# Attention with memory feeding a gated expert layer: the first group of tokens is made of two batches' ends, and attended tokens are transposed one pair of heads at a time

## Chip, cores and metric

One core of a Trainium2 chip. The metric is the device time of one execution in microseconds (us), taken as the median of several runs; lower is better.

## What is computed

```python
# attention with memory: B=4 batches, H=8 heads, S=576 tokens, D=64
scores = causal(scale * q @ k.T)              # per head, 576 x 576, masked
a = softmax(scores)
local = a @ v
mem_out = phi(q) @ M_prev / (phi(q) @ z_prev + 1e-6)
x = g * mem_out + (1 - g) * local             # g = sigmoid(beta), one number for each head
# expert layer over all 2304 tokens: d_model 512, d_ff 1536
x = x.transpose(0, 2, 1, 3).reshape(2304, 512)
out = (sigmoid(x @ w_gate) * (x @ w_val)) @ w_out
```

The expert weights arrive as 64-bit floats. The kernel turns each value into a sum of two 32-bit numbers (hi and lo) and multiplies with three products: hi*hi, hi*lo, lo*hi.

## The kernel before

The 2304 tokens are worked off in six **groups** of 384 tokens (`NG`, `GT`). Groups 0 to 3 are *plain*: the first 384 tokens of one batch each. Groups 4 and 5 are *tail* groups: the last 192 tokens of two batches each. In a group attention runs over four **pairs** of heads (n = 0 to 23 in all, four to a group). A pair has three items c, each of 128 tokens. In a plain pair the items see 128, 256 and 384 keys. In a tail pair items 0 and 1 see 512 keys and item 2, half from each batch, sees 576 (in pieces of 320 and 256).

For each item `scores` (line 447) multiplies queries with keys on TensorE, takes the masked maximum on VectorE (L481) and the exponential on ScalarE (L490). `turn` (495) transposes the result on TensorE (L217) and ScalarE copies it out. After the third item `values` (514) multiplies with the values (L214); four small VectorE operations and one addition give `xs`. `memory` (402) is the memory term (L214, VectorE). Scores come in two forms: pairs n < `SPLIT` = 9 multiply 32-bit numbers directly, with 64 rows to a head (L469); from pair 9 on `split` (426) makes hi and lo parts on ScalarE and VectorE (`kq`, `ql`), and TensorE takes two full-height products to a head (L477 and L478 by the helper on L210).

`across` (540) turns the finished tokens of a **whole group** so that the model dimension lies on partitions. For each of three token blocks it does four transposes, one ScalarE cast of 512 columns (`xh`) and one VectorE subtraction (`xl`). It runs after the group's fourth pair.

`moe` (656) is the expert layer of a group: for each of 12 slices f of d_ff it does 24 matmuls of 384 columns (12 for the gate, 12 for the value, on `xh` and `xl`), the *gate* on ScalarE and VectorE (tanh L694, product L696, cast, subtraction), and, one slice later, 9 matmuls of 512 columns into three accumulators (`down`). The accumulators are copied out by ScalarE (`ob`, L711) and stored. In the first group's layer the weights are loaded and converted (`convert`, 603): three thirds to a slice, each with two ScalarE and five VectorE operations of 512 columns (L611, L613, L616, L619, L233). The ring `sv` has three buffers, so conversion runs at most two slices ahead of use. Later groups read the converted weights back.

The order on each engine is made by `Program.issue` (96): every operation is recorded with a cost, and a list scheduler with fixed costs writes out one queue for each engine, by the order of recording where several operations are ready. At run time each queue is worked off in its order. First all of group 0's attention is recorded (`weights(0)` and `weights(1)` at two of its steps), then the layer of group g with the attention of group g + 1 woven in between (`SPREAD`). While group 0 is in attention all eight PSUM banks serve it; afterwards three do.

Of the kernel before, what the change touches and what calls it, by code (L numbers as in the profile page):

```python
# [21 lines left out]
VC = 66  # L22
# [123 lines left out]
def tile_attention_memory_moe(  # L146
# [75 lines left out]
    def copy(out, in_, n, r, w):  # L222
        act(n, lambda: nc.scalar.copy(out=out, in_=in_), r, w)  # L223
# [78 lines left out]
    vr_r = Ring("vr", [128, 5, 2, VC], F32, 2)  # L302
    vt_r = Ring("vt", [128, 5, 2, VC], F32, 2, {0: ("wr0", ("wr", 0)), 1: ("wr1", ("wr", 1))})
    kp_r = Ring("kp", [128, 2 * GT], F32, 4)
# [11 lines left out]
    class Pair:  # L316
        pass

    def batches(g):
        return [g] if g < B else [2 * (g - B), 2 * (g - B) + 1]  # L320

    def items_of(g):

        return [(128 * c, 128 * c + 128) for c in range(3)] if g < B else [(0, 512), (0, 512), (64, S)]

    pairs = []
    for g in range(NG):
        for p in range(HP):
            u = Pair()
            u.g, u.p, u.tail, u.bs = g, p, g >= B, batches(g)  # L330
# [8 lines left out]
    xs_t = {}  # L339

# [173 lines left out]
    def values(n):  # L514
# [5 lines left out]
        with pg.block():  # L520
            for c in range(3):
# [10 lines left out]
        if u.g not in xs_t:  # L532
            xs_t[u.g] = xs_r.take()
        xs, xk = xs_t[u.g]
        x = xs[:, :, 2 * u.p:2 * u.p + 2]
        k = xk + (u.p,)
        scaled(x, [k], pv, tk, rs_r, 1e-9, ga[:, 2 * u.p:2 * u.p + 2], "ga")
        tt(nc.vector, ALU.add, x, x, u.xm, GT, [k] + u.xm_k, [k])

    def across(g, c):  # L540

        xs, xk = xs_t[g]
        if g not in x_t:
            x_t[g] = [xh_r.take(), xl_r.take(), []]
        (xh, xh_k), (xl, xl_k), keys = x_t[g]
        tp, tk = bank("att")
        x = xs[:, c].rearrange("p h d -> p (h d)")
# [3 lines left out]
        src = tp.rearrange("p (a q) -> p a q", a=KD)  # L551
        hi, lo = xh[:, :, c * 128:c * 128 + 128], xl[:, :, c * 128:c * 128 + 128]
        kh, kl = xh_k + (c,), xl_k + (c,)
        copy(hi, src, DM, [tk], [kh])
        sub(nc.vector, lo, src, hi.bitcast(F32), DM, [tk, kh], [kl])
        keys += [kh, kl]

    seq = [(n, c) for n in range(NP) for c in range(3)]

    def attn():  # L560
# [6 lines left out]
        for t in range(len(seq) + SKEW):  # L567
# [15 lines left out]
            if t >= SKEW:  # L583
                n, c = seq[t - SKEW]
                turn(n, c)
                yield
                if c == 2:
                    values(n)
                    load_values(n + 2)
                    yield  # L590
                    if n % HP == HP - 1:
                        g = pairs[n].g
                        for c in range(3):
                            across(g, c)
                            yield
                        yield ("group", g)

# [50 lines left out]
    def rows(g, t):  # L648
        if g < B:
            return [(g * S + t * 128, 0, 128)]  # L650
        b = 2 * (g - B)
        if t < 2:
            return [((b + t) * S + GT, 0, 128)]
        return [((b + e) * S + GT + 128, 64 * e, 64) for e in range(2)]

    def moe(g):
# [16 lines left out]
        for f in range(NF):  # L673
            cur = ready_w.pop(g * NF + f)
            pz = []
            for part in range(2):
                pp, pp_k = bank("gv")
                pz.append((pp, pp_k))
                (wh, wh_k), (wl, wl_k) = cur[part]
                n = 0  # L680
                for kd in range(KD):
                    o = slice(kd * 128, kd * 128 + 128)
                    for (l, l_k), r in (((wh, wh_k), xh), ((wh, wh_k), xl), ((wl, wl_k), xh)):
                        matmul(pp[:, :GT], l[:, o], r[:, kd], GT, [l_k] + xk, [pp_k],
                               n == 0, n == 3 * KD - 1)
                        n += 1
                    if kd % 2 == 1:
                        yield
            th, th_k = th_r.take()
# [33 lines left out]
    def count(g):  # L723

        return HP * 9 + 4

# [82 lines left out]
```

## Time and profile before

| | |
|---|---|
| runs | 705.32, 705.69, 705.99 us; median 705.69 us |
| profiled execution | 704.67 us, of which the profile's span is 702.9 us |
| TensorE (PE) busy | 672.7 us, 96% of the span |
| VectorE (DVE) busy | 369.8 us, 53% |
| ScalarE (ACT) busy | 340.3 us, 48% |
| GpSimd (POOL) busy | 8.0 us, 1% |
| DMA | 122.20 MB, mean 174 GB/s |

An engine's busy share is a mean over the span; it hides that DVE is busy nearly all the time in the first quarter and a third of it at the end. "PEclk" is the clock that TensorE was granted, as a share of 2.4 GHz: 1.00 is 2.4 GHz, 0.50 is 1.2 GHz, and values between are stretches of both. A matmul's listed duration overlaps the next one's, so the cost of one in a stream is read from start to start.

### The profile page before, as it was taken

To read this page: it belongs to the slowest core of one execution; us is meant where nothing else is said; L and a number is where in the kernel's file an instruction comes from. 1 tells how busy PE (TensorE), PEld (TensorE's weight loads), DVE (VectorE), ACT (ScalarE), POOL (GpSimd) and SP (SyncE) were. 2 spreads that over 40 slices of the span, in tenths; PEclk is the share of its full clock that TensorE was granted. 3 is DMA by queue.
4 is the path that set the end of the run, shared out by engine and by line. 5 is a ranking of instruction groups with operands and counts; after the bars stand their busy time and mean duration, and the time that the engine had idled before them with its cause. 6 is when DMAs were issued, how large, how long until landed. Compare 5 with 4: busy or idle time off the path is not lost.

```text
span 702.9 us, 12510 instructions
## 1 busy us (share of the span) xinstructions
PE 672.7 (96%) x4992; PEld 598.0 (85%) x4992; DVE 369.8 (53%) x1005; ACT 340.3 (48%) x666; POOL 8.0 (1%) x52
## 2 busy tenths in 40 slices
PE   4997999998999999999999999999999999999996
PEld 3564888777899999999998988989898889999995
DVE  5866999989654444453545355363634532311111
ACT  6664565557645526543546366373736533221111
POOL 2000000000000000000000000000000000000000
PEclk9976999999999999999999999999999999999999
DMA  8654668776744345544537335534631423454542
GB/s 269 215 167 154 210 221 280 245 260 233 281 154 158 148 142 189 202 153 149 185 120 253 116 124 185 147 133 160 223 136 70 159 66 117 126 219 179 180 152 73
DMA packets 31946, 122.20 MB, mean 174 GB/s; under 512 B 7568, under 2 KB 9616, under 8 KB 22672
## 3 DMA queue, kind: packets, MB, share of 16 engines
q1 hardware_dynamic: 31888, 121.41, 49.9%
q8 instruction: 39, 0.64, 0.4%
q14 instruction: 19, 0.16, 0.1%
HBM read 104.09 MB, written 17.30 MB: 173 GB/s over the span
## 4 chain that ended last, share of the span: by engine, by line
PE 88%; ACT 5%; DVE 4%; DMA 1%; issue 1%; POOL 1%; POOLq 0%; SPq 0%; ACTq 0%; DVEq 0%
PE bank L210 68%; PE bank L214 10%; PE bank L217 7%; PE bank L469 3%; ACT kq L223 2%; ACT a L490 1%; DMA mb<-in_mz_dram 1%; DVE wt L616 1%; DVE wt L619 1%; ACT at L223 0%; DVE a L481 0%; DVE wt L611 0%; DVE wt L613 0%; DMA out_dram<-ob 0%; DVE xs L233 0%
## 5 line engine op out<-in xcount | busy, mean ns | idle before, releaser
L210 PE MATMUL bank<-xh,wg 128*128 128x384 f32 x576 | 168.9, 349 | 2.6 <-ACT wg L223 2.2
L210 PE MATMUL bank<-xh,sv 128*128 128x384 f32 x576 | 170.1, 348 | 0.0
L210 PE MATMUL bank<-sv,gh 128*128 128x512 f32 x432 | 140.7, 403 | 0.4 <-ACT gh L223 0.4
L210 PEld LDWEIGHTS bank<-xh,wg 128*128 128x128 f32 x576 | 107.0, 191 | 10.3 <-issue 3.3
L210 PEld LDWEIGHTS bank<-xh,sv 128*128 128x128 f32 x576 | 106.2, 188 | 3.1 <-issue 1.4
L696 DVE SCALAR_TENSOR_TENSOR th<-th,bank 128x384 f32<-128x384 f32 x72 | 39.8, 553 | 118.8 <-PE bank L210 117.6
L481 DVE CUSTOM_DVE_ANT_0 a<-bank,mask 128x128 f32<-128x128 f32 (+3 forms) x144 | 66.5, 486 | 66.8 <-PE bank L210 54.1
L490 ACT ACTIVATE a<-a,st 128x128 f32<-128x128 f32 (+3 forms) x144 | 79.8, 581 | 42.2 <-DVE st L481 41.2
L210 PE MATMUL bank<-xl,wg 128*128 128x384 f32 x288 | 99.2, 344 | 0.0
L210 PE MATMUL bank<-xl,sv 128*128 128x384 f32 x288 | 98.9, 343 | 0.0
L694 ACT ACTIVATE th<-bank 128x384 f32<-128x384 f32 x72 | 35.2, 489 | 116.1 <-PE bank L210 115.7
L210 PEld LDWEIGHTS bank<-sv,gh 128*128 128x128 f32 x432 | 78.2, 188 | 14.1 <-issue 1.4
L210 PE MATMUL bank<-sv,gl 128*128 128x512 f32 x216 | 86.6, 401 | 0.0
L223 ACT CAST gh<-th 128x384 fp32r<-128x384 f32 x72 | 36.8, 512 | 99.1 <-DVE th L696 98.8
L223 ACT COPY at<-bank 128x512 f32<-128x512 f32 (+1 forms) x120 | 59.0, 514 | 35.9 <-PE bank L217 34.5
L217 PE MATMUL bank<-idn,a 128*128 128x128 f32 x400 | 72.4, 282 | 3.1 <-ACT a L490 2.9
L223 ACT CAST kq<-kp 64x768 fp32r<-64x768 f32 (+1 forms) x92 | 56.0, 615 | 16.5 <-PE bank L210 15.2
L217 PEld LDWEIGHTS bank<-idn,a 128*128 128x128 f32 x400 | 51.3, 145 | 13.7 <-ACT a L490 5.8
L210 PEld LDWEIGHTS bank<-xl,wg 128*128 128x128 f32 x288 | 55.1, 191 | 2.6
L210 PEld LDWEIGHTS bank<-xl,sv 128*128 128x128 f32 x288 | 54.3, 189 | 0.6 <-issue 0.2
L233 DVE TENSOR_TENSOR gl<-th,gh 128x384 fp32r<-128x384 f32 x72 | 40.0, 556 | 22.4 <-ACT gh L223 21.9
L210 PEld LDWEIGHTS bank<-sv,gl 128*128 128x128 f32 x216 | 40.6, 188 | 9.4 <-issue 0.3
(62 smaller groups left out, 723.4 us busy)
## 6 DMA issues: line engine op xcount, KB each, us to landing
sv<-w SPq DMA_DIRECT2D x60, 1024.0 KB, 4.8
wr<-in_w_dram SPq DMA_DIRECT2D x36, 512.0 KB, 4.1
kp<-in_qk_dram SPq DMA_DIRECT2D x32, 384.0 KB, 4.3
w<-sv SPq DMA_DIRECT2D x12, 1024.0 KB, 5.4
out_dram<-ob SPq DMA_DIRECT2D x16, 256.0 KB, 3.9
vr<-in_vp_dram SPq DMA_DIRECT2D x16, 198.0 KB, 4.6
vt<-in_vp_dram SPq DMA_DIRECT2D x8, 330.0 KB, 3.5
vr<-in_vp_dram SPq DMA_DIRECT2D x8, 330.0 KB, 3.1
```

Source lines behind the costliest of these rows:

```text
L210: lambda: nc.tensor.matmul(out=out, lhsT=lhsT, rhs=rhs, start=start, stop=stop), r, w)
L214: lambda: nc.tensor.matmul(out=out, lhsT=lhsT, rhs=rhs, start=start, stop=stop), r, w)
L217: pe(0.110, lambda: nc.tensor.transpose(out=out, in_=in_, identity=identity), r, w)
L223: act(n, lambda: nc.scalar.copy(out=out, in_=in_), r, w)
L233: dve(n, lambda: nc.vector.tensor_tensor(out=out, in0=in0, in1=in1, op=op), r, w)
L469: pe(2 * m / 2385.0, lambda kp=kp, j=j, r=r, q=q, m0=m0, m1=m1: nc.tensor.matmul(out=sp[j][0][m0:m1, :m], lhsT=kp[r, u.qa + q:u.qa + q + m ...
L481: dve(m + 60, lambda aj=aj, sj=sj, pj=pj: nc.vector.tensor_tensor_reduce(out=aj[:, k0:k1], in0=pj[:, :m], in1=mk, scale=-0.125, scalar=3.0 ...
L490: act(W, lambda aj=aj, sj=sj: nc.scalar.activation(out=aj[:, :W], in_=aj[:, :W], func=AF.Exp, scale=-1.0, bias=sj[:, len(ns) - 1:len(ns)], ...
L616: dve(DM, lambda: nc.vector.scalar_tensor_tensor(out=t, in0=hi, scalar=-0x40000000, in1=t, op0=ALU.bitwise_and, op1=ALU.bitwise_or,), [wr_ ...
L619: dve(DM, lambda: nc.vector.scalar_tensor_tensor(out=t, in0=lo, scalar=29, in1=t, op0=ALU.logical_shift_right, op1=ALU.bitwise_or,), [wr_k ...
L694: act(GT, lambda: nc.scalar.activation(out=th, in_=pg_[:, :GT], func=AF.Tanh, scale=0.5), [pg_k], [th_k])
L696: dve(GT, lambda: nc.vector.scalar_tensor_tensor(out=th, in0=th, scalar=1.0, in1=pv[:, :GT], op0=ALU.add, op1=ALU.mult,), [th_k, pv_k], [t ...
```

## The change

Three things are changed, and lines move up by a few, so that L469 becomes L472, L481 becomes L484, L696 becomes L689.

1. The groups run in another order: `ids = [4, 0, 1, 2, 3, 5]`. The tail group of batches 0 and 1 comes first, then the four plain groups, then the other tail group. Which pairs use the direct form still goes by n < 9: before these were nine plain pairs, now four tail pairs and five plain pairs.
2. `across` runs after **each pair**, with three transposes, one cast and one subtraction of 384 columns. A pair's tokens fill one of the four parts kd of `xh` and `xl`. For f = 0 the layer's 24 matmuls are written so that kd = 0, 1, 2 of gate and value come first and the six of kd = 3 last, and each waits for its own part alone.
3. Buffers: `xs` is a ring of two small tiles in place of one large; values of even pairs go to `vt`, of odd pairs to `vr`, and `vt` no longer shares memory with the buffers of the raw weights.

```diff
-    vt_r = Ring("vt", [128, 5, 2, VC], F32, 2, {0: ("wr0", ("wr", 0)), 1: ("wr1", ("wr", 1))})
+    vt_r = Ring("vt", [128, 5, 2, VC], F32, 2)
-    xs_r = Ring("xs", [128, 3, H, D], F32, 1)
+    xs_r = Ring("xs", [128, 3, 2, D], F32, 2)
+    ids = [B, *range(B), *range(B + 1, NG)]
     def batches(g):
-        return [g] if g < B else [2 * (g - B), 2 * (g - B) + 1]
+        i = ids[g]
+        return [i] if i < B else [2 * (i - B), 2 * (i - B) + 1]
-            ring = vt_r if u.tail and n % 2 == 0 else vr_r
+            ring = vr_r if n % 2 else vt_r
-    def across(g, c):
+    def across(n):
...
-        for i in range(KD):
-            transpose(tp[:, i * 128:i * 128 + 128], x[:, i * 128:i * 128 + 128], idn,
-                      [xk + (i,), "idn"], [tk])
+        for c in range(3):
+            transpose(tp[:, c * 128:c * 128 + 128], u.x[:, c].rearrange("p j d -> p (j d)"), idn,
+                      [u.x_k, "idn"], [tk])
+        hi, lo = xh[:, u.p], xl[:, u.p]
...
-                    if n % HP == HP - 1:
-                        g = pairs[n].g
-                        for c in range(3):
-                            across(g, c)
-                            yield
-                        yield ("group", g)
+                    across(n)
+                    yield ("group", pairs[n].g) if n % HP == HP - 1 else None
...
+            turns = [(part, kd) for part in range(2) for kd in range(KD)]
+            if f == 0:
+                turns = [x for x in turns if x[1] < KD - 1] + [x for x in turns if x[1] == KD - 1]
...
-                        matmul(pp[:, :GT], l[:, o], r[:, kd], GT, [l_k] + xk, [pp_k],
-                               n == 0, n == 3 * KD - 1)
+                    matmul(pp[:, :GT], l[:, o], r[:, kd], GT, [l_k] + xk[kd], [pp_k],
+                           kd == 0 and i == 0, kd == KD - 1 and i == 2)
```

Three places where the queues differ. In the names `kp` is a pair's queries and keys, `a` the exponentials, `at` their transposes, `vr` and `vt` values, `mb` and `ph` the memory term, `wr` and `wt` raw weights in conversion, `wg` and `sv` converted ones, `th` the gate.

TensorE at the start of the program, before:

```order
L469 MATMUL bank_63<-kp_101 128x128
L469 MATMUL bank_64<-kp_101 128x128
L469 MATMUL bank_66<-kp_101 128x256
L469 MATMUL bank_67<-kp_101 128x256
L469 MATMUL bank_69<-kp_101 128x384
L469 MATMUL bank_70<-kp_101 128x384
L214 MATMUL bank_65<-mb_104,ph_105 128x130 x3
L217 MATMUL bank_68<-idn,a_107 128x128
L217 MATMUL bank_68<-idn,a_108 128x128
```

and now:

```order
L472 MATMUL bank_63<-kp_101 128x512
L472 MATMUL bank_64<-kp_101 128x512
L472 MATMUL bank_66<-kp_102 128x512
L472 MATMUL bank_67<-kp_102 128x512
L217 MATMUL bank_68<-idn,a_112 128x128 x4
L217 MATMUL bank_69<-idn,a_113 128x128 x4
L472 MATMUL bank_70<-kp_101 64x320
L472 MATMUL bank_63<-kp_101 64x320
L472 MATMUL bank_70<-kp_102 64x320
L472 MATMUL bank_63<-kp_102 64x320
```

The first pair's scores are of two batches (`kp_101`, `kp_102`) and of 512, 320 and 256 columns; the memory term, which waits for `mb`, comes 14 rows into the queue in place of six.

TensorE at the end of the first group, before, from the last pair's values to the layer's first matmuls:

```order
L214 MATMUL bank_65<-vr_106,at_136 64x66 x12
L217 MATMUL bank_70<-idn,a_118 128x128
L217 MATMUL bank_70<-idn,a_107 128x128
L469 MATMUL bank_69<-kp_101 128x384
L469 MATMUL bank_69<-kp_103 128x128
L217 MATMUL bank_66<-idn,xs_134 128x128
L217 MATMUL bank_67<-idn,xs_134 128x128
L217 MATMUL bank_68<-idn,xs_134 128x128
L469 MATMUL bank_68<-kp_101 128x256
L210 MATMUL bank_66<-xh_142,wg_89 128x384
L210 MATMUL bank_66<-xl_143,wg_89 128x384
```

and now, from the last pair's transposed tokens to the last six matmuls of f = 0 (the last pair's values end nine rows earlier, and ahead of those stand 18 of f = 0's 24 matmuls):

```order
L217 MATMUL bank_65<-idn,xs_143 128x128 x3
L472 MATMUL bank_69<-kp_102 128x256
L214 MATMUL bank_70<-vt_103,at_122 64x66 x4
L214 MATMUL bank_70<-vt_103,at_127 64x66 x8
L214 MATMUL bank_70<-vt_103,at_137 64x66 x3
L210 MATMUL bank_66<-xh_140,wg_89 128x384
L210 MATMUL bank_66<-xl_141,wg_89 128x384
L210 MATMUL bank_66<-xh_140,wg_89 128x384
L210 MATMUL bank_67<-xh_140,sv_128 128x384
L210 MATMUL bank_67<-xl_141,sv_128 128x384
L210 MATMUL bank_67<-xh_140,sv_128 128x384
```

Between the last transposes and the matmuls that need them there now stand a score matmul and the values of the next group's first pair (`vt_103`).

VectorE at the same place, before:

```order
L233 TENSOR_TENSOR xs_134<-xs_134,xm_131 128x3x128
L616 SCALAR_TENSOR_TENSOR wt_140<-wr_127,wt_140 128x512
L613 TENSOR_SCALAR wt_126<-wt_126 128x512
L619 SCALAR_TENSOR_TENSOR wt_140<-wr_127,wt_140 128x512
L233 TENSOR_TENSOR xl_143<-bank_66,xh_142 128x4x128
L233 TENSOR_TENSOR xl_143<-bank_67,xh_142 128x4x128
L233 TENSOR_TENSOR xl_143<-bank_68,xh_142 128x4x128
```

and now, with the first gate (`th`) behind it:

```order
L233 TENSOR_TENSOR xs_143<-xs_143,xm_135 128x384
L398 TENSOR_SCALAR rn_136<-bank_70 128x6
L400 RECIPROCAL rn_136<-rn_136 128x6
L233 TENSOR_TENSOR rn_136<-rn_136,gs 128x6
L233 TENSOR_TENSOR xm_135<-bank_70,rn_136 128x384
L484 ISA a_118,st_120<-bank_69,mask 128x256
L484 ISA st_120 128x1
L233 TENSOR_TENSOR xl_141<-bank_65,xh_140 128x384
L391 SCALAR_TENSOR_TENSOR ph_126<-kp_106,ph_126 128x384
L689 SCALAR_TENSOR_TENSOR th_147<-th_147,bank_67 128x384
```

The last pair's `xl` is one subtraction of 384 columns in place of three of 512, with the next group's attention ahead of it in place of weight conversion.

## Rows read from the trace of the kernel before

**Rows 1.** Windows between first copies of finished accumulators; busy us (instructions), clock, DMA.

```profile
core 0: us, PE busy (x) PEld busy (x) DVE busy (x) ACT busy (x) POOL busy (x), PEclk, DMA share, GB/s
180.32:277.93 97.61, 97.61 (x724) 90.92 (x723) 48.77 (x143) 48.55 (x100) 0.43 (x4) 1.00 0.48 173
277.93:379.90 101.97, 101.97 (x739) 94.25 (x738) 50.48 (x139) 50.23 (x101) 0.46 (x4) 1.00 0.47 169
379.90:504.60 124.70, 123.26 (x1057) 112.07 (x1057) 62.31 (x167) 67.52 (x127) 0.93 (x8) 1.00 0.45 158
504.60:620.47 115.87, 114.83 (x1004) 105.30 (x1004) 44.76 (x120) 47.76 (x89) 0.47 (x4) 1.00 0.36 127
620.47:695.69 75.22, 75.22 (x397) 70.58 (x396) 13.37 (x24) 13.85 (x27) 0.00 (x0) 1.00 0.46 164
```

**Rows 2.** Windows of the early part, from DVE's first operation on.

```profile
5.49:30.68 25.19, 20.48 (x174) 14.11 (x174) 20.24 (x74) 19.07 (x44) 0.33 (x3) 1.00 0.78 248
30.68:46.00 15.32, 12.22 (x83) 8.02 (x79) 11.52 (x37) 8.91 (x18) 0.11 (x1) 0.68 0.66 220
46.00:61.93 15.93, 11.26 (x95) 7.39 (x93) 13.40 (x40) 8.44 (x18) 0.22 (x2) 0.82 0.39 118
61.93:73.72 11.79, 11.79 (x47) 9.52 (x47) 6.42 (x18) 5.90 (x13) 0.00 (x0) 0.64 0.48 167
73.72:175.27 101.55, 97.63 (x659) 81.41 (x657) 94.55 (x233) 62.08 (x121) 0.66 (x6) 0.98 0.73 246
175.27:180.32 5.05, 5.05 (x27) 3.62 (x27) 3.96 (x14) 4.27 (x9) 0.00 (x0) 1.00 0.72 188
```

**Rows 3.** Timeline of PE and DVE around 35 us: start us, us, engine, line, operation.

```profile
35.03 0.42 DVE L613 TENSOR_SCALAR wt<-wt 128x512 int32<-128x512 int32 x1
35.37 0.55 DVE L481 CUSTOM_DVE_ANT_0 a<-bank,mask 128x384 f32<-128x384 f32 x1
...
36.63 0.90 PE L217 MATMUL bank<-idn,a 128*128 128x128 f32 x3 [2.70 <-ACT a L490]
```

**Rows 4.** Timeline of PE at the end of the first group.

```profile
60.78 1.22 PE L469 MATMUL bank<-kp 64*128 64x256 f32 x2 [2.43 <-DVE xl L233]
61.93 0.69 PE L210 MATMUL bank<-xh,wg 128*128 128x384 f32 x1
```

**Rows 5.** Timeline of PE: direct scores and transposes in the first group's attention.

```profile
8.31 2.93 PE L469 MATMUL bank<-kp 64*128 64x128 f32 x12 [8.31 <-DMA kp<-in_qk_dram]
...
21.62 0.91 PE L469 MATMUL bank<-kp 64*128 64x384 f32 x2
22.46 0.66 PE L217 MATMUL bank<-idn,a 128*128 128x128 f32 x4
23.05 0.48 PE L469 MATMUL bank<-kp 64*128 64x128 f32 x2
```

**Rows 6.** Chain that ended last: start us, us; both heads' scores, eight transposes, tail memory and values.

```profile
80.70 0.85 PE bank L469 x4
...
353.10 0.87 PE bank L217 x8
...
381.89 1.03 PE bank L214 x8
...
387.56 3.18 PE bank L214 x104
```

**Rows 7.** Timeline of PE: split scores of a tail pair.

```profile
488.31 0.39 PE L210 MATMUL bank<-kq 128*128 128x512 f32 x1
488.54 0.40 PE L210 MATMUL bank<-kq,ql 128*128 128x512 f32 x1
```

**Rows 8.** Groups by form: VectorE's masked maximum, tail and plain.

```profile
L481 DVE CUSTOM_DVE_ANT_0 a<-bank,mask 128x512 f32<-128x512 f32 x32 | 21.1, 686 | 10.6 <-PE bank L210 10.3
L481 DVE CUSTOM_DVE_ANT_0 a<-bank,mask 128x256 f32<-128x256 f32 x32 | 12.6, 414 | 5.0 <-PE bank L210 4.4 <-ACT a L490 0.4
L481 DVE CUSTOM_DVE_ANT_0 a<-bank,mask 128x320 f32<-128x320 f32 x16 | 7.2, 488 | 19.7 <-PE bank L210 19.7
```

More of the change, by code (lines that the diff above doesn't have):

```diff
@@ L317, in tile_attention_memory_moe @@
         pass
+    ids = [B, *range(B), *range(B + 1, NG)]
     def batches(g):
-        return [g] if g < B else [2 * (g - B), 2 * (g - B) + 1]
+        i = ids[g]
+        return [i] if i < B else [2 * (i - B), 2 * (i - B) + 1]
     def items_of(g):
-        return [(128 * c, 128 * c + 128) for c in range(3)] if g < B else [(0, 512), (0, 512), (64, S)]
+        return [(128 * c, 128 * c + 128) for c in range(3)] if ids[g] < B else [(0, 512), (0, 512), (64, S)]
     pairs = []
@@ L329, in tile_attention_memory_moe @@
             u = Pair()
-            u.g, u.p, u.tail, u.bs = g, p, g >= B, batches(g)
+            u.g, u.p, u.tail, u.bs = g, p, ids[g] >= B, batches(g)
             u.nk = 5 if u.tail else 3
@@ L338, in tile_attention_memory_moe @@
     x_t = {}
-    xs_t = {}
     def load_unit(g):
@@ L531, in values @@
                                     keys, [tk], i == 0, i == nb - 1)
[L532 to L538, printed above, removed]
-    def across(g, c):
[L542 to L545, printed above, removed]
-        tp, tk = bank("att")
-        x = xs[:, c].rearrange("p h d -> p (h d)")
-        for i in range(KD):
-            transpose(tp[:, i * 128:i * 128 + 128], x[:, i * 128:i * 128 + 128], idn,
-                      [xk + (i,), "idn"], [tk])
[L551 to L556, printed above, removed]
+        u.x, u.x_k = xs_r.take()
+        scaled(u.x, [u.x_k], pv, tk, rs_r, 1e-9, ga[:, 2 * u.p:2 * u.p + 2], "ga")
+        tt(nc.vector, ALU.add, u.x, u.x, u.xm, GT, [u.x_k] + u.xm_k, [u.x_k])
+    def across(n):
+        u = pairs[n]
+        if u.p == 0:
+            x_t[u.g] = [xh_r.take(), xl_r.take(), []]
+        (xh, xh_k), (xl, xl_k), keys = x_t[u.g]
+        tp, tk = bank("att")
+        for c in range(3):
+            transpose(tp[:, c * 128:c * 128 + 128], u.x[:, c].rearrange("p j d -> p (j d)"), idn,
+                      [u.x_k, "idn"], [tk])
+        hi, lo = xh[:, u.p], xl[:, u.p]
+        kh, kl = xh_k + (u.p,), xl_k + (u.p,)
+        copy(hi, tp[:, :GT], GT, [tk], [kh])
+        sub(nc.vector, lo, tp[:, :GT], hi.bitcast(F32), GT, [tk, kh], [kl])
+        keys.append([kh, kl])
     seq = [(n, c) for n in range(NP) for c in range(3)]
@@ L648, in rows @@
     def rows(g, t):
-        if g < B:
-            return [(g * S + t * 128, 0, 128)]
-        b = 2 * (g - B)
+        b = batches(g)[0]
+        if ids[g] < B:
+            return [(b * S + t * 128, 0, 128)]
         if t < 2:
@@ L674, in moe @@
             cur = ready_w.pop(g * NF + f)
[L675 to L678, printed above, removed]
-                (wh, wh_k), (wl, wl_k) = cur[part]
[L680 to L683, printed above, removed]
-                        matmul(pp[:, :GT], l[:, o], r[:, kd], GT, [l_k] + xk, [pp_k],
-                               n == 0, n == 3 * KD - 1)
-                        n += 1
-                    if kd % 2 == 1:
-                        yield
+            pz = [bank("gv") for _ in range(2)]
+            turns = [(part, kd) for part in range(2) for kd in range(KD)]
+            if f == 0:
+                turns = [x for x in turns if x[1] < KD - 1] + [x for x in turns if x[1] == KD - 1]
+            for n, (part, kd) in enumerate(turns):
+                pp, pp_k = pz[part]
+                (wh, wh_k), (wl, wl_k) = cur[part]
+                o = slice(kd * 128, kd * 128 + 128)
+                for i, ((l, l_k), r) in enumerate((((wh, wh_k), xh), ((wh, wh_k), xl), ((wl, wl_k), xh))):
+                    matmul(pp[:, :GT], l[:, o], r[:, kd], GT, [l_k] + xk[kd], [pp_k],
+                           kd == 0 and i == 0, kd == KD - 1 and i == 2)
+                if n % 2 == 1:
+                    yield
             th, th_k = th_r.take()
@@ L723, in count @@
     def count(g):
-        return HP * 9 + 4
+        return HP * 10
     constants()
```

## The prediction

> **What bounds the kernel.** I began with the time from one group's first accumulator copy to the next, since the change swaps whole groups. From 180.32 us on TensorE has nearly no gap: in each window its busy time is within 1.5 us of the window and the clock is 1.00 [rows 1]. There the kernel lasts as long as its matmuls. The five windows read as 75.2 us of expert layer (the last one, which has no attention woven in) plus the next group's attention: 97.61 and 101.97 us with a plain group, 124.70 and 115.87 with a tail group. So a plain group's attention is worth (97.61 + 101.97)/2 - 75.2 = 24.6 us there and a tail group's (124.70 + 115.87)/2 - 75.2 = 45.1 us.
>
> The early part is another matter [rows 2]. From 5.49 to 73.72 us, where VectorE does the first gate's product, VectorE is busy 20.24 + 11.52 + 13.40 + 6.42 = 51.6 of 68.2 us and TensorE 55.8, but part of that at 1.2 GHz: the granted clock is 0.68, 0.82 and 0.64 in three of the four windows. Two places show why. At 35 us VectorE works through weight conversion before it takes a masked maximum; ScalarE's exponential waits for that, and TensorE waits 2.70 us for ScalarE [rows 3]. At the end of the group TensorE waits 2.43 us behind VectorE's `xl`, and the layer begins at 61.93 us [rows 4]. From 73.72 to 175.27 us (first to twelfth gate) VectorE is busy 94.55 and TensorE 97.63 of 101.55 us: both are nearly full.
>
> **The late part.** Behind the first group's layer stand now three windows with a plain group and one with a tail group, in place of two and two. One tail attention, 45.1 us, goes out and a plain one, 24.6, comes in: **-20.5 us**. The last window (75.2) and what follows it stay, since a tail group is still last. The turning costs nothing here: the transposes are 72 as before, four casts and subtractions of 384 columns replace three of 512, and ScalarE and VectorE are busy only half of these windows [rows 1]. Without that cover it would be some tenths of a microsecond a group.
>
> **The early part** gets those matmuls instead, in the direct form. I sum what the new queues place ahead of the first gate.
>
> TensorE, one tail pair. A direct score group takes 0.84 us from start to start for 384 columns (21.62 to 22.46 us, one head) [rows 5], and 0.85 us for both heads when they stand next to each other [rows 6]. With 128 columns it is 0.41. I draw a line through these: 0.21 plus 0.21 for each 128 columns, so 1.05 for 512, 0.74 for 320, 0.63 for 256. No trace row shows two batches' 64-row halves next to each other. They could run together, as the two heads do, or singly; I take together, because a tail pair's values, half of which alternate so between batches at 64 columns, take 3.18/104 = 31 ns an instruction [rows 6]. In the new queue the four pairs' scores are then 12 groups of 512, 9 of 320 and 8 of 256: 24.3 us. Run singly they would be 16 of each, 38.7; I keep +14 for the upper end. A pair has besides 1.03 of memory, 3.18 of values and 26 + 3 transposes at 0.87/8 = 0.109 [rows 6]: 7.4. Four pairs: 24.3 + 29.6 = 53.9. The queue has also f = 0's 24 matmuls, at 0.175 (4.2), and the next plain pair with the beginning of another, about 8.5. Sum **66.6 us** from 8.31 us on, when the first queries land [rows 5]: **74.9 us** at the earliest.
>
> VectorE. To the old 51.6 us come, for four pairs, two heads each of 0.686 + 0.686 + 0.488 and about 0.48 in place of 0.414, 0.55 and 0.28, which lie on the line through 256 and 512 columns [rows 8], 1.09 x 8 = 8.7 us; two and a half more thirds of a conversion ahead of the first gate (11 finished in the new queue, 9 in the old) at an estimated 2.5 us (five operations, two of 0.34 [rows 3] and three of 0.6, as 512 columns are), 6; and a further pair's beginnings, 4. Overlaps of 0.08 a row [rows 3] take 1 off. Sum 69 from 5.49: **74.5 us**. So the two engines need the same time, where before they needed 57 (VectorE) and 49 (TensorE, the same sum over the old queue, 40.3 from 8.31), and the first gate came at 73.72, 17 us late.
>
> How late will it be now? About 9 of the 17 us belong to the end of the group: some 4 of idle time ahead of 61.93 and then 61.93 to 73.72 at a clock of 0.64, which costs about 4 more. There the changed queue has 18 of f = 0's 24 matmuls ahead of the last pair, and no triple `xl`. The other 8 lie over 45 us of group 0 and should grow with its length (66.6 against 40.3): 13. I take **14, so the first gate at 89 us**, with ends at 5 (80 us) and at 26 (101).
>
> From first to twelfth gate VectorE's queue holds 82 us in place of 93 (two or three thirds and more attention are already done), TensorE's 88 in place of 89, by the same durations. TensorE loses 12 us there now, 4 of them idle late in the window behind a full VectorE; I take **94 us** (89 to 98). With the 5.05 us that follow [rows 2] the first accumulator copy comes at 89 + 94 + 5 = 188 us, 7.7 later.
>
> In this are further edits. The split form leaves four tail pairs (512 columns take two products of 0.23 us a head [rows 7], by columns 3.9 us a pair) and comes to four plain ones; by the direct form a tail pair costs 6.1, so +8.7, and four plain pairs go from some 3.1 (1.9 where the heads stand together, 3.8 where they don't) to 1.4, so -6.8: together +1.9, which the sums above and the unchanged window lengths already carry to within 1 us. DMA: a tail pair brings four loads of 384 and 330 KB in place of two, about 3.4 MB more for the group, and on SyncE's queue they stand ahead of `mb`, so the memory term starts some 3 us later; 14 queue rows of TensorE cover most of it. The DMA share there is 0.78 and 0.66, the bytes find room; if not, `wr` lands late and ScalarE's first conversion step with it. I price that within the 14.
>
> **Sum**: +7.7 - 20.5 = -12.8 us on the profiled execution, 704.67 to 691.9. The median of the runs is 1.0 above that execution; I predict **692.9 us**.
>
> A page's rule speaks against the change. The row: four transposes take 0.59 us to the next start when 64-row scores follow [rows 5], against 0.44 by the rate of [rows 6], so going from one shape to the other costs about 0.15. The Trainium skill (TensorEngine Tiling (Array Packing), Key Properties) says that changing the tiling mode drains TensorE. By that rule the 15 additional changes ahead of the first gate (60 in the new queue, 45 in the old) are 2 us more early, and the 27 fewer behind it give 4 back; by the rows both are in the 0.21 above already.
>
> **Rivals.**
> *The early part runs at TensorE's old pace* (slower). Before, the first gate took 65.4 us from 8.31 for 40.3 us of matmuls, 1.62 each. If that ratio holds, because every pair passes TensorE, VectorE, ScalarE and TensorE again with one item of lead, then 66.6 x 1.62 + 8.3 = 116 us, the first copy at 215 and the run at 719. It decides from a first gate at about 102 us on (704.7). For it: the waits of [rows 3], which the change doesn't remove. Against it: the ratio is that of a queue with 40 us of matmuls against 50 of VectorE. Chance 0.15.
> *The same lateness as before.* 25 us behind TensorE's sum gives a first gate at 100 and 703.5 on the profiled scale, 704.5 on the median: no change. Chance 0.06. Near it lies that the turning by pairs saves nothing, since the last six matmuls of f = 0 still wait for the last pair: plus 8, a run of 700.5; this is in my forecast's range.
> *TensorE stays busy and at full clock.* First gate at 80, then 89 us: first copy at 174, the run 678 to 679. For it: the clock fell to 0.68 after the wait of [rows 3] and to 0.64 after that of [rows 4], and stood at 1.00 in every window where TensorE was full [rows 1]; the new first group has twice the matmuls. The Trainium skill (TensorE: Matmul & The Clock Gate, The HAM clock gate) says that the throttled clock is the default and activity releases it, which would bring this case about; the trace agrees in both directions. Chance 0.17.
>
> **Numbers.** My forecast (684 to 703) has 0.62. The range 680 to 704 leaves out most of the slow rival and part of the fast one. About 0.2% of the time, 1.4 us, is what a measurement can tell from no change. Faster: 0.62 + 0.17 = 0.79; within 0.2%: 0.06; slower: 0.15.
>
> **What would show it.** Right: windows behind the first copy of about 98, 102, 100, 118 and 75 us; a first gate between 80 and 101 us; layer matmuls of f = 0 ahead of the last pair's transposes and no wait for `xl` over 1 us; VectorE near 90% busy to the first gate. Wrong: a first gate past 102 us, or a clock at half for 30 us of the early part (then the rival of the old pace); a late part that saves other than 19 to 22 us (then the swap was mispriced); two batches' score halves that run singly (0.74 us for each 320-column matmul).

## The result and the profile after

The changed kernel takes **686.73 us** (median of four runs, 686.13 to 687.59) against 705.83 (705.32 to 705.99) for the kernel before in the same session: a ratio of 0.9737 (95% interval 0.9723 to 0.975), 19.1 us less. The prediction was 692.9 us, with a range of 680 to 704. The profiled execution took 686.17 us, of which 684.4 are the span.

From the page of the changed kernel: the totals, and two of the forty-slice strips.

```profile
span 684.4 us, 12496 instructions
PE 663.3 (97%) x4992; PEld 582.0 (85%) x4992; DVE 363.1 (53%) x995; ACT 334.3 (49%) x656; POOL 8.1 (1%) x52
DVE  6799889898864443454444345454445533111111
PEclk9999999999999999999999999999999999999999
```

The reader is to see the last strip: the granted clock is at 0.9 or more of 2.4 GHz in every slice. VectorE is busy for 60% and more of each of the first twelve slices, and for half or less of those behind them.

The windows of the changed kernel, cut at the same events as [rows 1, 2]: first gate, twelfth gate, first accumulator copy, and the first copies of the five layers that follow.

```profile
core 0: us, PE busy (x) PEld busy (x) DVE busy (x) ACT busy (x) POOL busy (x), PEclk, DMA share, GB/s
5.49:85.44 79.95, 72.36 (x762) 46.20 (x763) 70.17 (x212) 58.28 (x116) 1.42 (x12) 1.00 0.76 253
85.44:178.76 93.32, 92.29 (x573) 77.07 (x572) 84.29 (x206) 60.37 (x117) 0.33 (x3) 1.00 0.70 234
178.76:182.78 4.02, 4.02 (x60) 3.32 (x59) 3.86 (x10) 2.00 (x4) 0.00 (x0) 1.00 0.59 210
182.78:285.39 102.61, 102.52 (x744) 93.75 (x743) 51.10 (x152) 50.65 (x105) 0.54 (x5) 1.00 0.47 164
285.39:383.50 98.11, 98.11 (x722) 91.00 (x721) 45.03 (x132) 46.92 (x96) 0.43 (x4) 1.00 0.45 163
383.50:485.90 102.40, 102.40 (x739) 94.00 (x738) 50.07 (x140) 50.47 (x101) 0.47 (x4) 1.00 0.49 171
485.90:601.37 115.47, 114.68 (x1004) 105.27 (x1004) 45.24 (x121) 48.13 (x90) 0.47 (x4) 1.00 0.35 128
601.37:677.13 75.76, 75.65 (x397) 70.60 (x396) 13.35 (x24) 13.73 (x27) 0.00 (x0) 1.00 0.46 163
```

| stretch | before, us [rows 1, 2] | after, us | change | forecast |
|---|---|---|---|---|
| start to first gate | 73.72 | 85.44 | +11.7 | +15.3 |
| first to twelfth gate | 101.55 | 93.32 | -8.2 | -7.6 |
| to the first accumulator copy | 5.05 | 4.02 | -1.0 | 0 |
| five late windows | 515.4 | 494.4 | -21.0 | -20.5 |
| behind the last first copy | 7.2 | 7.3 | +0.1 | 0 |
| span | 702.9 | 684.4 | -18.5 | -12.8 |

Cut at the first copy, the late part gave what the swap was priced at, and the early part, which took in a tail group in place of a plain one, grew by only 2.5 us and not by 7.7. The cut matters: at the second copy the change is 7.5 us behind (285.39 to 277.93), and the four windows left give 26.0, so the division between the parts is uncertain by some 5 us; their sum is not. VectorE is busy 158.3 us from 5.49 us to the first copy (70.17 + 84.29 + 3.86) where it was 150.1 [rows 2], and idle 19.0 in place of 24.7.

The timeline of TensorE in the changed kernel (start us, us, engine, line, operation; in brackets the idle time ahead of it and what ended that):

```profile
26.55 1.92 PE L217 MATMUL bank<-idn,a 128*128 128x128 f32 x15 [1.35 <-ACT a L493]
28.41 0.75 PE L472 MATMUL bank<-kp 64*64 64x320 f32 x2
29.09 3.25 PE L214 MATMUL bank<-vt,at 128*64 128x66 f32 x104
32.27 0.76 PE L472 MATMUL bank<-kp 64*64 64x320 f32 x6
32.96 0.44 PE L217 MATMUL bank<-idn,a 128*128 128x128 f32 x2
...
64.26 0.42 PE L210 MATMUL bank<-xh,wg 128*128 128x384 f32 x1
...
81.84 0.55 PE L217 MATMUL bank<-idn,xs 128*128 128x128 f32 x3 [0.55 <-DVE xs L233]
82.31 0.70 PE L472 MATMUL bank<-kp 64*128 64x256 f32 x2
```

Three things of the forecast are here. The wait for an exponential is 1.35 us where [rows 3] had 2.70. A tail pair has four score products of 320 columns, one for each head of each batch, and the trace shows each as two instructions. One product alone takes 0.68 us to the next start (28.41 to 29.09), and three together, more than one batch's two heads, take 0.69 (32.27 to 32.96). So the two batches' halves run side by side. And the layer begins at 64.26 us, 17.6 us ahead of the last pair's transposes at 81.84. These wait 0.55 us for `xs`; behind them TensorE has no wait for `xl`, where [rows 4] had 2.43.

### The profile page after: what moved, and what is told of

Read it like the earlier page. It is cut to its first block, busy times and chain, and to the rows that moved or that the text cites. A ratio compares the mean times of both kernels' runs of the same rounds, so it can differ in the third digit from the quotient of the medians.

```text
span 684.4 us, 12496 instructions
## 1 busy us (share of the span) xinstructions
PE 663.3 (97%) x4992; PEld 582.0 (85%) x4992; DVE 363.1 (53%) x995; ACT 334.3 (49%) x656; POOL 8.1 (1%) x52
## 4 chain that ended last, share of the span: by engine, by line
PE 90%; ACT 5%; DMA 2%; DVE 1%; issue 1%; SPq 1%; POOL 0%; ACTq 0%
PE bank L210 70%; PE bank L214 10%; PE bank L217 7%; PE bank L472 4%; ACT a L493 1%; ACT kq L223 1%; DMA vt<-in_vp_dram 1%; ACT at L223 1%; DMA kp<-in_qk_dram 1%; SPq L241 1%; DVE a L484 0%; ACT wt L603 0%; DMA out_dram<-ob 0%; ACT ob L704 0%; DVE xs L233 0%
## 5 line engine op out<-in xcount | busy, mean ns | idle before, releaser
L210 PE MATMUL bank<-xh,wg 128*128 128x384 f32 x576 | 166.0, 343 | 0.3
L210 PE MATMUL bank<-sv,gh 128*128 128x512 f32 x432 | 142.6, 407 | 0.0
L689 DVE SCALAR_TENSOR_TENSOR th<-th,bank 128x384 f32<-128x384 f32 x72 | 39.8, 553 | 145.3 <-PE bank L210 130.7
L210 PEld LDWEIGHTS bank<-xh,wg 128*128 128x128 f32 x576 | 105.1, 188 | 7.8 <-issue 2.9
L493 ACT ACTIVATE a<-a,st 128x512 f32<-128x512 f32 (+4 forms) x144 | 79.8, 581 | 44.7 <-DVE st L484 43.7
L484 DVE CUSTOM_DVE_ANT_0 a<-bank,mask 128x512 f32<-128x512 f32 (+4 forms) x144 | 66.5, 485 | 55.6 <-PE bank L210 49.3
L217 PEld LDWEIGHTS bank<-idn,a 128*128 128x128 f32 x400 | 49.7, 142 | 15.0 <-ACT a L493 4.9
L223 ACT CAST kq<-kp 64x768 fp32r<-64x768 f32 (+1 forms) x76 | 48.2, 638 | 16.4 <-PE bank L210 15.2
L472 PE MATMUL bank<-kp 64*128 64x512 f32 (+5 forms) x156 | 42.1, 494 | 9.4 <-DMA kp<-in_qk_dram 8.4
L233 DVE TENSOR_TENSOR gl<-th,gh 128x384 fp32r<-128x384 f32 x72 | 39.9, 554 | 20.5 <-ACT gh L223 20.1
```

The lines of the kernel that those rows point to most:

```text
L210: lambda: nc.tensor.matmul(out=out, lhsT=lhsT, rhs=rhs, start=start, stop=stop), r, w)
L217: pe(0.110, lambda: nc.tensor.transpose(out=out, in_=in_, identity=identity), r, w)
L233: dve(n, lambda: nc.vector.tensor_tensor(out=out, in0=in0, in1=in1, op=op), r, w)
L472: pe(2 * m / 2385.0, lambda kp=kp, j=j, r=r, q=q, m0=m0, m1=m1: nc.tensor.matmul(out=sp[j][0][m0:m1, :m], lhsT=kp[r, u.qa + q:u.qa + q + m ...
L484: dve(m + 60, lambda aj=aj, sj=sj, pj=pj: nc.vector.tensor_tensor_reduce(out=aj[:, k0:k1], in0=pj[:, :m], in1=mk, scale=-0.125, scalar=3.0 ...
L493: act(W, lambda aj=aj, sj=sj: nc.scalar.activation(out=aj[:, :W], in_=aj[:, :W], func=AF.Exp, scale=-1.0, bias=sj[:, len(ns) - 1:len(ns)], ...
```

## The experiments

Twelve further kernels were run in three sessions. The kernel before ran in each (medians 705.71, 705.41 and 705.02 us), and each ratio is against it. The rows shown of a run are of one execution; with the turning alone, VectorE's added work in the changed kernel, GpSimd and the buffers alone, it was the longest of that run, 2.9, 1.9, 8.7 and 3.7 us above the median. Two questions lead through them: which edit brought the time, and which engine paces the early part. In the second question **V** is the theory that VectorE's work does, **P** that TensorE's queue does (T in two of the recorded expectations).

**Order alone.** The new order and the new value buffers, with the old turning of a whole group; to make room in memory the rings `th` and `ph` have one buffer in place of two.

```diff
+    ids = [B, *range(B), *range(B + 1, NG)]
...
-            ring = vt_r if u.tail and n % 2 == 0 else vr_r
+            ring = vr_r if n % 2 else vt_r
```

> The new order of groups with the old turning of a whole group at its end (the tiles ph and th lose one of two buffers to make room). Theory A (the swap takes 20.5 us out of the part that is bound by TensorE, and the early part grows little because TensorE's new work fills time that it spent waiting behind VectorE's conversions): about 692 us, 11 to 16 below the kernel before; the end of the first group comes back, with a wait of about 5 us ahead of the first layer matmul and perhaps some us at the half clock. Theory B (the order gives nothing by itself, early growth eats the late saving, and the gain is that of turning pair by pair): 703 to 706 us. Late windows of about 102, 98, 102, 116, 75 us by both.

688.06 us (687.3 to 688.74), ratio 0.9751 (0.9737 to 0.9766). The interval overlaps the full change's: without the turning by pairs nearly all of the gain is there. What of it belongs to the buffers, a later run shows. Its windows (columns as above), to the first gate, to the twelfth, and the end of its first group:

```profile
5.49:87.89 82.40, 74.15 (x738) 47.73 (x740) 69.47 (x209) 57.44 (x111) 1.64 (x12) 0.94 0.71 238
87.89:179.49 91.60, 91.60 (x642) 78.61 (x638) 83.28 (x207) 57.39 (x112) 0.44 (x4) 1.00 0.71 242
60.00:85.44 25.44, 22.06 (x185) 15.80 (x183) 19.99 (x61) 14.94 (x31) 0.68 (x4) 0.80 0.67 222
```

With whole-group turning the clock still falls at the group's end (0.80 from 60 to 85 us), and the first gate comes 2.4 us later than in the change (87.89 to 85.44). At the twelfth gate 0.7 us of it are left (179.49 to 178.76), since the next stretch is shorter.

**Turning alone.** The full change, with the groups in their old order.

```diff
-    ids = [B, *range(B), *range(B + 1, NG)]
+    ids = list(range(NG))
```

> The old order of groups with turning pair by pair and the reordered f = 0. Theory A: 696 to 701 us; the wait at the end of the first group goes (4 to 5 us) and with it the half clock from 57 to 72 us (4 to 5 us), while the wait at 35 us with its half clock stays, and so do the late windows of 98, 102, 125, 116, 75 us. Theory B: 687 to 690 us. A third theory, C (the clock is what counts, and it falls wherever attention alone has too few matmuls): the clock still falls in both places, 702 to 706 us.

709.83 us (707.89 to 712.73), ratio 1.0066 (1.0039 to 1.0093): slower than before. So the turning by pairs does not bring the gain, and with the old order it costs. From here the new order alone takes off 23.1 us (709.83 to 686.73). Its windows, from 30 to 60 us and to the two gates:

```profile
30.00:60.00 30.00, 25.90 (x157) 17.41 (x157) 19.25 (x66) 15.74 (x34) 0.32 (x2) 0.60 0.47 151
5.49:72.06 66.57, 55.37 (x372) 37.91 (x373) 48.34 (x159) 39.49 (x85) 1.18 (x8) 0.79 0.57 186
72.06:179.53 107.47, 104.37 (x627) 82.73 (x626) 95.36 (x239) 67.11 (x130) 0.72 (x3) 0.98 0.68 237
```

The first gate comes only 1.7 us earlier than before, with the clock at 0.60 for 30 us (0.77 there in the kernel before), and VectorE has done 3 us less by then, which the next stretch pays for.

**The order of f = 0 undone.** The full change without the rearranged 24 matmuls.

```diff
-            if f == 0:
-                turns = [x for x in turns if x[1] < KD - 1] + [x for x in turns if x[1] == KD - 1]
```

> The changed kernel without the reordering of f = 0's 24 matmuls: each still waits for its own part of the tokens alone. Theory A: 0 to 2 us slower than the changed kernel (686.7), since nine of the 24 can still stand ahead of the last pair and the queue has the next group's attention to fill with. Theory B: 4 us or more slower, since the first six waits come back.

687.07 us (684.97 to 689.97), ratio 0.9741 (0.9713 to 0.9768). No difference from the full change can be measured.

**The tail group second.** `ids = [0, B, 1, 2, 3, B + 1]`, the rest as changed.

> The changed kernel with the tail group as the second group in place of the first: its attention is woven into the first layer. Theory A: what counts is the work that TensorE gets while the first group is in attention, before any layer matmul is there; that time stays as in the kernel with the turning alone, and the first layer's window can only give back the 4 to 5 us that TensorE idles late in it: 3 to 6 us below the kernel with the turning alone, 691 to 697 us. Theory D (it is enough that tail attention lies anywhere beside the conversions): within 2 us of the changed kernel, 685 to 689 us.

697.4 us (694.76 to 702.7), ratio 0.9894 (0.9842 to 0.9947): about 10.7 us slower than with the tail group first, though the late part is equally relieved (495.6 us from the first copy to the last first copy, and 494.4 in the change). From its windows, to the first gate, to the twelfth, and to the first accumulator copy:

```profile
5.49:68.01 62.52, 51.95 (x383) 35.08 (x384) 49.28 (x162) 39.38 (x84) 0.91 (x8) 0.95 0.64 208
68.01:186.98 118.97, 118.97 (x889) 92.77 (x887) 105.39 (x256) 78.69 (x146) 0.68 (x6) 1.00 0.70 239
186.98:193.22 6.24, 6.24 (x117) 4.98 (x115) 4.66 (x12) 2.86 (x6) 0.00 (x0) 1.00 0.67 245
```

TensorE has no gap between the gates (118.97 of 118.97 us). Ahead of the first gate it has 10.6 us of idle time, some 2.8 of them until the first queries land, and a plain group's matmuls leave it so. The place of the tail group decides.

**Both tail groups first.** `ids = [B, B + 1, 0, 1, 2, 3]`, the rest as changed.

> The changed kernel with both tail groups first, then the four plain ones. The second tail group's attention then lies beside the first layer's conversions; its 8 pairs take the direct form, one plain pair too. Theory P (in the changed kernel TensorE is the pace in the early part too: it idles only 5.7 us from its first matmul to the first accumulator copy): nothing is left to fill, the direct form of four more tail pairs costs some 3 us, late waits for the split of a tail pair go: 684 to 690 us. Theory V (VectorE still is the pace there, with 158 of 177 us busy): the early part has room for 20 us more of TensorE work at the cost of the tail pairs' VectorE work alone, about 8 us: 672 to 680 us.

682.44 us (681.42 to 683.1), ratio 0.9679 (0.9652 to 0.9706): the fastest kernel here, 4.3 us under the change. From its windows, between the gates, the last layer with attention, and the last layer:

```profile
88.50:202.63 114.13, 114.11 (x957) 91.50 (x957) 96.27 (x234) 72.36 (x136) 0.69 (x6) 1.00 0.66 228
505.41:599.20 93.79, 93.79 (x686) 86.82 (x685) 32.67 (x93) 30.60 (x64) 0.00 (x0) 1.00 0.39 144
599.20:675.00 75.80, 75.69 (x397) 70.62 (x396) 13.34 (x24) 13.74 (x28) 0.00 (x0) 1.00 0.45 163
```

The first copy comes at 208.98 us, 26.2 later than with one tail group in front, and the five late windows take 466.0 us, 28.3 less. The change as a whole, with the first tail group in front, had moved that copy by 2.5 us: between the gates TensorE is now full, and little is hidden any more. What is left of the gain is mostly the difference of two nearly equal numbers.

**VectorE's work up by 12 us, in the changed kernel.** The first of a conversion's integer steps is preceded by one further, idempotent step (36 more of the operation on L604).

```diff
+        dve(DM, lambda: nc.vector.tensor_scalar(
+            out=tf, in0=tf, scalar1=F64_TINY, scalar2=None, op0=ALU.max), [t_k], [t_k], fast=True)
```

> The changed kernel with the first VectorE step of each conversion third done twice (the same maximum again, which changes nothing in the result): 36 x 0.34 = 12 us more of VectorE work, all in the early part. Theory P: 0 to 4 us slower, 687 to 691 us. Theory V: 8 to 12 us slower, 695 to 699 us.

698.69 us (696.73 to 700.58), ratio 0.991 (0.9878 to 0.9943): 12.0 us over the change.

**TensorE's work up by 11.5 us, in the changed kernel.** The matmuls of the memory term are done three times for pairs 0 to 3 and twice for pairs 4 to 7.

```diff
+            for _ in range((3 if n < 4 else 2) if n < 8 else 1):
```

> The changed kernel with the memory products of the first four pairs done three times and those of the next four twice (the same product again into the same place): 4 x 2 x 1.03 + 4 x 0.81 = 11.5 us more of TensorE work, all in the early part. Theory P: 9 to 12 us slower, 695 to 699 us. Theory V: 0 to 4 us slower, 687 to 691 us.

690.34 us (689.71 to 690.64), ratio 0.9791 (0.9766 to 0.9816): 3.6 us over the change. The windows to the two gates, with more VectorE work first:

```profile
5.49:91.58 86.09, 78.15 (x750) 49.16 (x752) 71.30 (x220) 58.14 (x114) 1.44 (x12) 0.96 0.66 221
91.58:192.44 100.86, 96.52 (x585) 79.14 (x584) 93.65 (x234) 61.25 (x117) 0.33 (x3) 0.98 0.65 224
```

and with more TensorE work:

```profile
5.49:89.11 83.62, 79.37 (x824) 53.57 (x826) 70.69 (x212) 58.75 (x115) 1.60 (x12) 1.00 0.70 234
89.11:183.44 94.33, 94.33 (x603) 79.29 (x598) 84.39 (x207) 58.99 (x116) 0.33 (x3) 1.00 0.69 233
```

By the ranges stated ahead V is met (12.0 us for 12) and P is not (3.6 us for 11.5). But neither run changed one thing alone: the list scheduler wrote new queues. The windows to the twelfth gate of the direct score matmuls alone (L472; L473 with more TensorE work) show it, for the changed kernel, with more VectorE work and with more TensorE work (PE, PEld, clock, DMA):

```profile
5.49:178.76 173.27, 40.47 (x152) 13.71 (x152) 1.00 0.73 242
5.49:192.44 186.95, 45.91 (x152) 15.55 (x152) 0.97 0.65 223
5.49:183.44 177.95, 37.33 (x152) 12.82 (x152) 1.00 0.69 233
```

The same 152 instructions take 40.5, 45.9 and 37.3 us. With more VectorE work TensorE is busy 174.7 us for as many matmuls as took 164.7, at a clock of 0.97, and idle 12.3 in place of 8.6. So most of the 13.7 us by which the twelfth gate is late are longer TensorE work, and not waiting. With more TensorE work the memory products take 23.2 us in place of 9.6, but the whole busy time grows only to 173.7, since other matmuls became shorter, and idle time falls to 4.3. The time follows VectorE's work more closely than TensorE's in these two runs; that VectorE by itself sets the pace is not shown.

**The same two on the kernel before**, with 12 us of VectorE work and 10 us of TensorE work.

> The kernel before with the first VectorE step of each conversion third done twice, 36 x 0.34 = 12 us more of VectorE work in the early part. Theory V (VectorE was the pace of the old early part too): 8 to 12 us slower, 714 to 718 us. Theory T (TensorE, with its waits and its half clock, was the pace): 0 to 4 us slower, 706 to 710 us.

717.45 us (715.25 to 720.36), ratio 1.0185 (1.0146 to 1.0224): 12.4 us more.

> The kernel before with the memory products of the first four pairs done three times and of the next four twice, 12 x 0.83 = 10 us more of TensorE work in the early part. Theory V: 0 to 5 us slower, 706 to 711 us; it may even gain if the added work keeps the clock from falling. Theory T: 10 us or more slower, 716 to 720 us.

702.28 us (701.47 to 703.64), ratio 0.9969 (0.9956 to 0.9983): with ten microseconds of needless matmuls the kernel is 0.3% faster. Its windows to the two gates and from 30 to 60 us, and for the last the kernel before:

```profile
5.49:73.71 68.22, 57.03 (x450) 42.36 (x451) 54.72 (x176) 43.99 (x94) 0.73 (x6) 0.87 0.63 206
73.71:168.47 94.76, 93.77 (x660) 79.83 (x659) 88.62 (x220) 60.44 (x115) 0.55 (x5) 1.00 0.74 254
30.00:60.00 30.00, 23.57 (x235) 17.16 (x234) 25.68 (x80) 19.67 (x41) 0.33 (x3) 0.88 0.54 178
```

```profile
30.00:60.00 30.00, 23.02 (x194) 15.53 (x190) 23.67 (x75) 17.14 (x38) 0.33 (x3) 0.77 0.49 158
```

From 30 to 60 us the clock is granted at 0.88 in place of 0.77, and VectorE gets 25.7 us of work done where it did 23.7. Whether the clock is the cause or the moved schedule was not separated.

**A VectorE step moved.** The last subtraction of a conversion goes to GpSimd, in the changed kernel.

```diff
-        sub(nc.vector, lo_out, tf, hi_out.bitcast(F32), DM, [t_k, kh], [kl])
+        sub(nc.gpsimd, lo_out, tf, hi_out.bitcast(F32), DM, [t_k, kh], [kl])
```

> The changed kernel with the last step of each conversion third, 36 subtractions of 0.69 us, on GpSimd in place of VectorE: 25 us of VectorE's work leave the early part, GpSimd is idle there. Theory P: at most the 5.7 us of TensorE idle can come back, 682 to 687 us. Theory V: 8 to 15 us less, 671 to 679 us. If GpSimd's subtractions come late to the matmuls that need them, a few us slower by either.

696.37 us (694.72 to 705.06), ratio 0.9869 (0.9836 to 0.9903): slower than the change by 9.6 us. Groups of this kernel by form (busy us, mean ns of one, idle time ahead):

```profile
L235 POOL TENSOR_TENSOR sv<-wt,sv 128x512 fp32r<-128x512 f32 x24 | 35.0, 1465 | 70.4 <-ACT sv L223 58.5 <-issue 11.9
L609 DVE SCALAR_TENSOR_TENSOR wt<-wr,wt 128x512 int32<-128x512 int32 x36 | 31.2, 870 | 0.5
```

and of the changed kernel:

```profile
L609 DVE SCALAR_TENSOR_TENSOR wt<-wr,wt 128x512 int32<-128x512 int32 x36 | 24.5, 685 | 0.1
L233 DVE TENSOR_TENSOR sv<-wt,sv 128x512 fp32r<-128x512 f32 x24 | 16.1, 685 | 0.5 <-ACT sv L223 0.4
```

Some 25 us leave VectorE (36 x 0.685), but its other four steps become longer and give 17 back (L609 685 to 870 ns, L612 684 to 834, L604 420 to 533, L606 421 to 447, 36 of each), and the step itself takes 1465 ns on GpSimd in 24 of the 36. These five steps then last 4.1 us in place of 2.9. Further operations are longer too, and on the pages VectorE is busy 369.9 us in place of 363.1: it was not relieved at all. So this run does not tell V from P. That the length of a conversion from end to end sets the early pace is a rival that no run tests by itself. The Trainium skill (SBUF — State Buffer, Who interferes with whom) says that a VectorE instruction with two SBUF inputs contends with a GpSimd instruction that reads SBUF; L609 and L612 have two such inputs, and the trace agrees. It names L604's kind too, for modes that this trace doesn't show.

**Buffers alone.** The kernel before, with the new assignment of value buffers and `th` and `ph` at one buffer each, as in the run of the order alone.

```diff
-    vt_r = Ring("vt", [128, 5, 2, VC], F32, 2, {0: ("wr0", ("wr", 0)), 1: ("wr1", ("wr", 1))})
+    vt_r = Ring("vt", [128, 5, 2, VC], F32, 2)
...
-            ring = vt_r if u.tail and n % 2 == 0 else vr_r
+            ring = vr_r if n % 2 else vt_r
```

> The kernel before with the buffers of the run that had the new order alone: values in rings of their own, taken in turn by even and odd pairs, and one buffer each for th and ph. It tells whether that run's gain is the order's. If it is: 703 to 708 us, no change. If the buffers carry it: below 700 us.

700.7 us (699.67 to 704.39), ratio 0.9941 (0.992 to 0.9962): 0.6% faster with the old order and the old turning. This is net of what the single buffers of `th` and `ph` may cost. Plain pairs now have four value buffers in place of two, and `vt` no longer shares memory with raw weights; which of the two counts was not separated.

**Turning, with every layer matmul waiting for all four pairs** and f = 0 not rearranged, in the old order of groups: the waits of before, the turning of after.

```diff
-                    matmul(pp[:, :GT], l[:, o], r[:, kd], GT, [l_k] + xk[kd], [pp_k],
+                    matmul(pp[:, :GT], l[:, o], r[:, kd], GT, [l_k] + [k for ks in xk for k in ks], [pp_k],
```

> The old order with turning pair by pair, but f = 0 in its old order and each of its matmuls waiting for all four pairs, so that no layer matmul can go ahead of the first group's attention. Theory V says of the slow run with turning alone (709.8) that matmuls which nobody waited for went ahead of attention on TensorE at the half clock, and VectorE got its work later: without them 702 to 707 us. The rival, that turning by pairs is itself dearer: 708 to 712 us.

708.06 us (median of ten runs, 704.36 to 711.75 and one of 716.56 that the ratio leaves out), ratio 1.0048 (1.0022 to 1.0074). This overlaps the run of the turning alone (1.0039 to 1.0093). That matmuls of f = 0 which start too early keep TensorE from what VectorE needs is therefore not borne out.

## Why the prediction was right, and where it was not

**The late part: right.** The windows were forecast at about 98, 102, 100, 118 and 75 us and came to 102.6, 98.1, 102.4, 115.5 and 75.8; their sum fell by 21.0 us for a forecast of 20.5. The parts balance: the plain windows came to 303.1 us for 300, the tail window to 115.5 for 118. TensorE is busy within 1 us of each window, as in [rows 1], so the price of a group could be read from windows alone.

**The two floors: VectorE's right, TensorE's too low.** VectorE's sum to the first gate was 69 us, and its busy time there is 70.17. One term was small: a conversion's five VectorE operations were taken at 2.5 us and are 2.9 (420 + 421 + 685 + 684 + 685 ns by form). Two batches' score halves run together, as assumed. TensorE's sum was 66.6 us, and it is busy 72.36. Mis-sized were above all the transposes, priced at 0.109 us by a row of eight: fifteen take 1.86 us to the next start (26.55 to 28.41) and three 0.47 (81.84 to 82.31), 0.124 and 0.157 each. The four of [rows 5], 0.59 us, had said so: the 0.15 that the prediction found for a change of shape was said to be in the 0.21 already, but that term belongs to scores.

**Sound as a total, wrong in its parts: the lateness.** 14 us behind the sum of 74.9 were taken; 10.5 were measured (85.44 - 74.9), and 5.8 of these are the matmul time missing in the sum, so 4.7 are idle time of TensorE. That is 3.5 of the 5.7 us by which the span was missed; 1.0 lies in the stretch ahead of the first copy, 0.6 between the gates, 0.5 in the late windows. The step that failed is the one that said where the lateness comes from: "About 9 of the 17 us belong to the end of the group", to be saved by turning pairs, and "the other 8" to grow with the group to 13. By this the turning was worth some 8 us in all ("the turning by pairs saves nothing ... plus 8, a run of 700.5"), and the order alone would give 5. (692.9 + 8 is 700.9; and the rival with the same lateness comes to 702.9 by its own terms, not 703.5.) The medians say otherwise:

| step | us | ratio to before | interval |
|---|---|---|---|
| before (medians of the three sessions) | 705.0 to 705.7 | 1 | |
| + buffers | 700.7 | 0.9941 | 0.992 to 0.9962 |
| + order of groups | 688.06 | 0.9751 | 0.9737 to 0.9766 |
| + turning by pairs and order of f = 0 | 686.73 | 0.9737 | 0.9723 to 0.975 |

In this sequence the order is worth some 1.9% (13 us), the buffers 0.6% (4 us), which the prediction gave no price at all, and the turning nothing that can be measured. (The last step also gives `th` and `ph` their second buffer back.) The prices belong to the sequence: in the old order the turning costs 9 us against the buffers alone (709.83 to 700.7), and the order is then worth 23. The end of the group does cost time, 2.4 us at the first gate, but the stretch to the twelfth gate makes up for most of it (91.60 us and 93.32). One large error on the order's cost and one on the turning's gain stood against each other, and the buffers, taken at nothing, are about the rest: that the total came so close is partly luck.

**Why the order costs less early than it saves late: in part argued.** The prediction added TensorE's and VectorE's sums and took the longer one, with both at 75 us. The stretch up to the first copy, in the kernel before, with the buffers alone, with the order and the buffers, and in the change:

```profile
5.49:180.32 174.83, 158.44 (x1073) 124.08 (x1074) 150.09 (x413) 108.67 (x221) 1.32 (x12) 0.92 0.68 225
5.49:176.00 170.51, 155.53 (x1057) 121.31 (x1057) 148.44 (x408) 106.69 (x214) 1.50 (x12) 0.95 0.68 235
5.49:182.89 177.40, 168.74 (x1387) 128.59 (x1388) 156.04 (x421) 118.19 (x229) 2.08 (x16) 0.97 0.71 242
5.49:182.78 177.29, 168.66 (x1388) 126.58 (x1389) 158.32 (x427) 120.65 (x235) 1.75 (x15) 1.00 0.73 242
```

From before to after TensorE is busy 10.2 us more and idle 7.8 less, and its clock goes from 0.92 to 1.00; VectorE is busy 8.2 us more and idle 5.8 less. So a part of the tail group's matmuls filled gaps, and a part was paid by the clock; how much each was not separated. The 2.5 us are not the price of the tail group alone: with the buffers equal (second and third line) it is 6.9 us at the first copy and 9.2 at the second (277.25 to 286.46), though the second line is of that run's longest execution. In the runs with added work the time follows VectorE's more closely than TensorE's (12.0 and 12.4 us for 12, against 3.6 for 11.5 and 2.7 gained for 10), with queues and clocks that changed too. Where no gaps are, a tail group costs its matmuls: second in the order 10.7 us of the gain are lost, and a second tail group in front moves the first copy by 26.2 us.

**The clock: the fast rival's part that came true.** The granted clock is 1.00 in every window of after, where [rows 2] had 0.64 to 0.82 from 30.68 to 73.72 us. The Trainium skill's statement that activity releases the throttled clock (TensorE: Matmul & The Clock Gate, The HAM clock gate), with which the prediction supported this rival at 0.17, agrees with it. Its times did not come: it had the gates at 80 and 169 us, and they came at 85.44 and 178.76. The result lies between it and the forecast. The other two rivals needed a first gate at 100 us or later.

**Open.** Why turning by pairs, at most neutral in the new order, makes the old order slower (1.0066 against 0.9941 for the buffers alone): the one cause that was tried, early matmuls of f = 0, was not confirmed. A single step's part of a profiled execution is also uncertain by some microseconds, since attention of the next pairs moves across the border at the first copy: the run with more matmuls in the kernel before reaches that copy 8.0 us earlier (172.34 to 180.32), and ends 3.3 us earlier.

## What to carry to other kernels

Work for the engine with gaps belongs in the stage that has them, and the first such move is the cheap one: here it cost some 7 to 9 us of the early part with the buffers equal, and the next 26. Busy shares of 90% (VectorE) and 99% (TensorE) between the gates do not tell which engine's work the time follows. Adding work to one engine and then to the other is a test of it, but only as far as the rest stays as it was: where a scheduler writes the queues anew, compare the durations of the untouched instructions too (here 152 score instructions took 37.3 to 45.9 us). An edit that comes along for room (two buffers that no longer share memory) needs a price of its own, and prices of edits need not add: the turning cost 9 us in one order of groups and nothing in the other.

## What was not expected of the hardware

- A kernel with 10 us of needless matmuls in the early part was 0.3% faster (0.9956 to 0.9983), with the granted clock at 0.88 in place of 0.77 from 30 to 60 us. Its queues were written anew too, so the clock's part is not known.
- GpSimd beside VectorE lengthened VectorE's operations by 6 to 27% (421 to 447 ns and 685 to 870 ns at the ends), and needed 1465 ns for most of the subtractions that VectorE does in 685.
